# Two-layer gated network after a decayed linear attention on one core: outer products inside the values' product, a late check of the decay, and other options for the planner

## The chip, the core and the metric

The kernel runs on one core of a Trainium2 chip. The metric is the device time of one execution in microseconds (us). The kernel before takes 942.81 us (median of 3 runs, 942.36 to 943.93).

## What is computed

Three parts follow each other; the sizes are 4 batches of 768 positions, 8 heads of 48, a model width of 384 and a hidden width of 2048.

```python
for t in range(S):                       # attention, state per batch and head: 48 x 48
    cur = einsum('bhd,bhe->bhde', u * kt, vt)
    y[:, :, t] = einsum('bhd,bhde->bhe', rt, state + cur)
    state = w * state + einsum('bhd,bhe->bhde', kt, vt)
x = y laid out as (3072 tokens, 384)
h = x @ w_in;  x = (h * tanh(softplus(h))) @ w_out          # first layer
h = x @ w2_in; P = a0 + a1*h + a2*h^2 + a3*h^3              # second layer
Q = 1 + |b0|*|h| + |b1|*h^2;  out = (P / (Q + 1e-6)) @ w2_out
```

## The kernel before, in words

The 768 positions are cut into 6 chunks of 128. A **unit** is one chunk of one batch, so there are 24 units (`unit`, L619). A unit loads `kraw`, `rraw`, `tr` and `tkv`, scales them with powers of the decay (`L630`, `L633`, `L635`, `L653`), makes scores (TensorE, L646), puts a diagonal into `am` (L660, L663) and the scores over it (VectorE, L668), multiplies with the state (L679) and the values (L685), copies the result `y` (L464 on ScalarE, L467 on VectorE), moves it by DMA into `xr` and splits it into a high and a low part (`xh`, `xl`) of the reduced float type in which TensorE multiplies. For all but the last four units, eight outer products (`kv`, L705) follow, which update the state `st` (VectorE, L714 or L717).

The network runs in **steps** (`step`, L760 on): one step is one block of 512 tokens and one slice of 128 of the 2048 hidden columns. There are 198 steps, numbered from 0 here; the first 12 have half a block (256 tokens). A step has nine matmuls into `h` (L779, "first product"), a chain of VectorE and ScalarE work that ends in a high part `gh` and a low part `gl`, and nine matmuls into the accumulators `acc` (L855, "second product"). In the first layer the chain is clip `e` (VectorE, L794), four activations (ScalarE, L798), the product `h` (VectorE, L800), `gh` (L464 on ScalarE or L467 on VectorE) and `gl` (VectorE, L804). In the second layer it is `x`, `v`, `yy` (ScalarE, L809 to L814), `v*x` (GpSimd, L817), `x` and `h` (ScalarE, L819, L827), the products L821 to L835 on VectorE, and a split into `gh` and `gl` (L464 to L467 and L483).

Weights arrive as pairs of 32-bit words and are converted: one scaling (L58 on ScalarE, L60 on GpSimd), three VectorE instructions (L64, L67, L71), and a split into `w` high (L464) and `w` low (L483). The 16 slices of the first layer are converted in the first 200 us or so, beside the units.

Nothing of this order is written by hand. `Plan` collects every operation with the engines that may run it and a guessed cost, and lists them greedily: for each operation it takes the engine that would end it first, where an option may carry a handicap (fourth entry, for example the 3.0 in `(V, tt(n), True, 3.0)`), and among operations that could start within 0.1 of the earliest it takes the highest rank (longest way to the end, plus a `boost`). The engines then execute the list in order. Where TensorE would stand idle early in the list, `order` puts **zero products** (`filler`, L848: 512 columns times zeros into the first accumulator) into the gap, up to planned time `FILL`:

```python
if self.filler is not None and self.filler.done and st < self.FILL:
    y = free.get(e, 0.0)
    while y + (0.22 if clock.full else 0.44) < st:
        y = clock(y, 0.216, 1.0)
        order.append(self.filler)
```

At the very start of the list `check_decay` (L897) loads the decays and tests with four VectorE instructions (L902 to L905) whether they lie in a range; the result `fin` is read at the program's end. All DMAs are issued by SyncE (L459). At the end, three copies `o` of the accumulators (ScalarE, L464) go out by three DMAs.

Of the kernel before, what the change touches and what calls it, by code (L numbers as in the profile page):

```python
# [250 lines left out]
class Plan:  # L251
# [6 lines left out]
    FILL = 30.0  # L258
# [137 lines left out]
def tt(n):  # L396
    return 0.07 + 1.04e-3 * n


def ts(n):  # L400
    return 0.07 + 0.52e-3 * n


def act(n, src=0.093):
    return src + 0.833e-3 * n


def ptt(n):
    return 0.149 + 2.1e-3 * n
# [6 lines left out]
def fast_path(tc, nc, d):  # L416
# [40 lines left out]
    def dma(dst, src, r=(), w=(), nbytes=196608, after=(), boost=0.0):  # L457

        return pl.add([(SP, 0.65 if nbytes == 98304 else 0.5)], lambda e: nc.sync.dma_start(out=dst(), in_=src()),  # L459
                      r=r, w=w, lat=0.757, after=after, move=nbytes / 3.6e5, boost=boost)  # L460
# [8 lines left out]
    PV = 0.3  # L469
# [147 lines left out]
    AHEAD, AHEAD1 = 40.0, 10.0  # L617

    def unit(U):  # L619
# [52 lines left out]
        pv, y, xr = n_ps(), n_y(), n_xr()  # L672

        def values(e):

            for j in range(4 if c else 0):
                for i in range(2):
                    rows = slice(64 * i, 64 * i + D)
                    x_ = nc.tensor.matmul(pv()[64 * i:64 * i + D, j * CH:(j + 1) * CH],  # L679
                                          lhsT=st()[rows, j * D:(j + 1) * D], rhs=rraw()[rows, j, :],  # L680
                                          start=(j == 0), stop=False)
            for j in range(4):
                for i in range(2):
                    h = 2 * j + i
                    x_ = nc.tensor.matmul(pv()[64 * i:64 * i + D, j * CH:(j + 1) * CH],  # L685
                                          lhsT=tkv()[:, 384 + h * D:384 + (h + 1) * D], rhs=am[i]()[:, j, :],
                                          start=(j == 0 and c == 0), stop=(j == 3))
            return x_
        pl.add([(T, 2.1 if c else 1.1)], values, r=[tkv, rraw] + ([st] if c else []) + am, w=[pv], boost=bo,
               rows=0.8)  # L690
        pl.add([(A, act(512, 0.052)), (V, tt(512))],
# [6 lines left out]
        if not last:  # L698
            kp = n_ps()

            def kv(e):
                for j in range(4):
                    for i in range(2):
                        h = 2 * j + i
                        x_ = nc.tensor.matmul(kp()[64 * i:64 * i + D, j * D:(j + 1) * D],  # L705
                                              lhsT=tkv()[:, h * D:(h + 1) * D], rhs=tkv()[:, 384 + h * D:384 + (h + 1) * D],
                                              start=True, stop=True)
                return x_
            pl.add([(T, 0.5)], kv, w=[kp], r=[tkv], boost=bo, rows=0.75)
# [55 lines left out]
    def step(s, after):  # L765
# [4 lines left out]
        xh, xl = xt[blk]  # L770
        parts = range(3) if l else range(4) if half is None else range(2 * half, 2 * half + 2)
# [18 lines left out]
        if l == 0:  # L790
# [11 lines left out]
            pl.add([(A, act(n, 0.052)), (V, tt(n))], lambda e: copy(e, ghs(), hp()), r=[h], w=[gh])  # L802
# [3 lines left out]
        else:  # L806
# [9 lines left out]
            pl.add([(G, ptt(n)), (V, tt(n), True, 3.0)],  # L816
# [20 lines left out]
            split(n, g, ghs, gls, g, (gh, gl))  # L837
# [23 lines left out]
        if final:  # L861
            for m in range(3):
# [21 lines left out]
                if l == 0:  # L884
                    dma(lambda m=m: x2d[cb]()[:, m, :], o, r=[o], w=[(x2d[cb], m)], nbytes=262144)
                else:
                    dma(lambda m=m: d["out"][cb, :, m, :], o, r=[o], nbytes=262144)
# [9 lines left out]
    def check_decay():  # L897
# [8 lines left out]
        pl.add([(V, 1.7)], fn, w=[f0, f1])  # L906

    setup()
    check_decay()
# [7 lines left out]
    for s, (blk, f, half, *_) in enumerate(steps):  # L917
# [11 lines left out]
        step(s, [end])  # L929
    with tc.manual_schedule():  # L930
# [81 lines left out]
```

## Time and profile before

| What | Value |
|---|---|
| median of 3 runs | 942.81 us |
| the profiled execution, its own time | 946.39 us |
| its span, first to last instruction | 944.4 us |
| TensorE busy (matmuls) | 907.2 us, 96% |
| VectorE busy | 705.2 us, 75% |
| ScalarE busy | 723.2 us, 77% |
| GpSimd busy | 527.7 us, 56% |
| mean granted TensorE clock | 0.977 of full speed |

How to read it: TensorE is near its limit over the span as a whole, but the shares of an average over stages with different limits don't tell which stage has time left. The tables by stage and the single rows that matter stand further down. Names: PE is TensorE, PEld its weight loads, DVE VectorE, ACT ScalarE, POOL GpSimd, SP SyncE.

### The profile page before, as it was taken

The page shows a single profiled execution, that of the slowest core. Times are in us where ns is not written, and L with a number is a line of the kernel's source. Part 1 is how long each engine was busy: PE and PEld are TensorE (multiplying, and loading weights), DVE is VectorE, ACT ScalarE, POOL GpSimd, SP SyncE. Part 2 cuts the span into 40 slices and gives each one's busy share as a digit, 9 for nine tenths or more (in the row PEclk, how much of TensorE's full clock was granted, in tenths as well). Part 3 has the DMA queues.
Part 4 walks back from the last instruction along what each step waited for, and adds up shares of the span by engine and source line. Part 5 has one row for each costly group of instructions (what it writes and reads, how often), then busy time and mean ns, then how long its engine had stood idle before and what let it go on. Part 6 is the DMA issues. An engine that isn't in the chain of part 4 may idle for free. (4 is left out here: it accounts for less than half of the span.)

```text
span 944.4 us, 13963 instructions
## 1 busy us (share of the span) xinstructions
PE 907.2 (96%) x5009; PEld 739.6 (78%) x5009; DVE 705.2 (75%) x1072; ACT 723.2 (77%) x1256; POOL 527.7 (56%) x464
## 2 busy tenths in 40 slices
PE   6689899999999999999999999999999999999995
PEld 4578687788788788778888878888888888888883
DVE  7988998795544554544568999987878887878883
ACT  3556777676677677767788998997988988979784
POOL 2548644641810750330065597786877886867663
PEclk8769999999999999999999999999999999999999
DMA  8755357431500520330045310020100100100001
GB/s 311 247 176 176 122 168 233 130 99 47 176 10 1 174 84 1 84 98 1 0 156 169 111 62 6 1 68 1 56 12 1 56 12 1 56 1 1 34 1 37
DMA packets 38576, 75.11 MB, mean 80 GB/s; under 512 B 4322, under 2 KB 16739, under 8 KB 38499
## 3 DMA queue, kind: packets, MB, share of 16 engines
q1 hardware_dynamic: 38498, 74.14, 24.5%
q8 instruction: 41, 0.67, 0.3%
q14 instruction: 37, 0.30, 0.1%
HBM read 58.40 MB, written 11.01 MB: 73 GB/s over the span
## 5 line engine op out<-in xcount | busy, mean ns | idle before, releaser
L855 PE MATMUL acc<-gh,w 128*128 128x512 f32 (+1 forms) x1188 | 391.3, 388 | 1.9 <-DVE gh L467 1.0
L779 PE MATMUL h<-xh,w 128*128 128x512 f32 (+1 forms) x960 | 318.3, 389 | 6.5 <-DVE w L483 3.5
L798 ACT ACTIVATE e<-e 128x512 f32<-128x512 f32 (+1 forms) x408 | 245.7, 606 | 42.5 <-DVE e L794 34.5
L855 PEld LDWEIGHTS acc<-gh,w 128*128 128x128 f32 x1188 | 223.3, 190 | 49.2 <-ACT gh L464 2.2
L855 PE MATMUL acc<-gl,w 128*128 128x512 f32 (+1 forms) x594 | 229.7, 387 | 5.5 <-DVE gl L804 2.9
L779 PEld LDWEIGHTS h<-xh,w 128*128 128x128 f32 x960 | 181.5, 191 | 45.8 <-DVE w L483 4.8
L779 PE MATMUL h<-xl,w 128*128 128x512 f32 (+1 forms) x480 | 184.7, 385 | 0.0
L483 POOL TENSOR_TENSOR gl<-yy,gh 128x512 fp32r<-128x512 f32 x96 | 125.4, 1308 | 46.6 <-ACT gh L464 31.4
L817 POOL TENSOR_TENSOR v<-v,x 128x512 f32<-128x512 f32 x96 | 124.7, 1302 | 31.5 <-ACT v L811 17.9
L855 PEld LDWEIGHTS acc<-gl,w 128*128 128x128 f32 x594 | 112.7, 190 | 29.3 <-DVE gl L804 3.5
L800 DVE SCALAR_TENSOR_TENSOR h<-e,h 128x512 f32<-128x512 f32 (+1 forms) x102 | 67.4, 661 | 86.7 <-ACT e L798 86.4
L779 PEld LDWEIGHTS h<-xl,w 128*128 128x128 f32 x480 | 92.1, 192 | 16.8
L794 DVE TENSOR_SCALAR e<-h 128x512 f32<-128x512 f32 (+1 forms) x102 | 67.0, 657 | 38.2 <-PE h L779 38.0
L464 ACT ACTIVATE gh<-h 128x512 fp32r<-128x512 f32 (+1 forms) x91 | 52.9, 581 | 49.8 <-DVE h L800 48.4
L819 ACT ACTIVATE x<-v,ceps 128x512 f32<-128x512 f32 x96 | 69.6, 725 | 17.9 <-POOL v L817 17.8
L804 DVE TENSOR_TENSOR gl<-h,gh 128x512 fp32r<-128x512 f32 (+1 forms) x102 | 67.0, 657 | 16.1 <-ACT gh L464 12.6
L811 ACT ACTIVATE v<-x,cf 128x512 f32<-128x512 f32 x96 | 78.4, 817 | 0.0
L779 PE MATMUL aps<-xh,w 128*128 128x512 f32 x228 | 75.7, 389 | 0.0
L719 POOL TENSOR_TENSOR st<-st,pw 128x192 f32<-128x192 f32 x16 | 9.1, 573 | 94.5 <-DVE st L717 94.5
L829 DVE SCALAR_TENSOR_TENSOR v<-v,ceps,h 128x512 f32<-128x512 f32 x58 | 43.3, 746 | 24.1 <-ACT h L827 23.8
L663 ACT ACTIVATE am<-dmk,dg 128x128 f32<-128x128 f32 x100 | 31.8, 392 | 24.0 <-DVE dg L638 24.0
L779 PEld LDWEIGHTS aps<-xh,w 128*128 128x128 f32 x228 | 42.8, 188 | 8.9
(104 smaller groups left out, 1352.2 us busy)
## 6 DMA issues: line engine op xcount, KB each, us to landing
wr<-in_w SPq DMA_DIRECT2D x32, 768.0 KB, 4.3
tkv<-in_tkv SPq DMA_DIRECT2D x24, 384.0 KB, 4.0
kraw<-in_kT SPq DMA_DIRECT2D x24, 256.0 KB, 2.7
rraw<-in_rT SPq DMA_DIRECT2D x24, 256.0 KB, 3.6
x<-o SPq DMA_DIRECT2D x24, 256.0 KB, 2.5
o<-x SPq DMA_DIRECT2D x24, 256.0 KB, 2.9
tr<-in_tr SPq DMA_DIRECT2D x24, 192.0 KB, 2.8
xr<-y SPq DMA_DIRECT2D x48, 96.0 KB, 3.6
```

Of the source, the lines that this page charges most:

```text
L464: return nc.scalar.activation(out=out, in_=x, func=AF.Copy)
L483: lambda e: eng[e].tensor_tensor(out=lo(), in0=x(), in1=hi().bitcast(F32), op=ALU.subtract),
L779: x_ = nc.tensor.matmul(h()[:, :n], lhsT=w()[:, a, m, :], rhs=x()[:, m, col:col + n], start=(i == 0), stop=(i == 8))
L794: pl.add([(V, tt(n))], lambda e: nc.vector.tensor_scalar(out=es(), in0=hp(), scalar1=20.0, scalar2=None, op0=ALU.min), r=[h], w=[e_])
L798: lambda e, func=func, kw=kw: nc.scalar.activation(out=es(), in_=es(), func=func, **kw), w=[e_])
L800: lambda e: nc.vector.scalar_tensor_tensor(out=hp(), in0=es(), scalar=-0.5, in1=hp(), op0=ALU.add, op1=ALU.mult), r=[e_], w=[h])
L804: lambda e: nc.vector.tensor_tensor(out=gls(), in0=hp(), in1=ghs().bitcast(F32), op=ALU.subtract),
L811: lambda e: nc.scalar.activation(out=v(), in_=x(), func=AF.Identity, scale=cf()[:, 5:6], bias=cf()[:, 4:5]), r=[x, cf], w=[v])
L817: lambda e: eng[e].tensor_tensor(out=v(), in0=v(), in1=x(), op=ALU.mult), r=[x], w=[v])
L819: lambda e: nc.scalar.activation(out=x(), in_=v(), func=AF.Ln, bias=ceps()), r=[v, ceps], w=[x])
L829: lambda e: nc.vector.scalar_tensor_tensor(out=v(), in0=v(), scalar=ceps(), in1=h(), op0=ALU.add, op1=ALU.mult), r=[h, ceps], w=[v])
L855: x_ = nc.tensor.matmul(ac[m]()[:, col:col + n], lhsT=w()[:, a, 3 + m, :], rhs=x()[:, :n], start=(first and i == 0 and s > 0), stop=(final ...
```

## The change

- The eight outer products `kv` are no operation of their own any more: they stand at the end of the function `values`, behind the values' products, in one planned TensorE operation.
- The options of the copy `y` and of the first layer's `gh` give VectorE a handicap of 1.0 (`VA`), so ScalarE is taken unless VectorE would end it 1.0 earlier.
- `check_decay` is added behind step 48 and waits for that step's second product.
- `FILL` goes from 30 to 75; the rank boost of the second chunk's units (`AHEAD1`) from 10 to 0; two cost guesses of VectorE from 0.07 to 0.08.
- In the last steps (`end`, by the code steps 195, 196 and 197) the handicap of VectorE for `v*x` and for `gl` falls from 3.0 to 0.0 and 0.3.
- The second of the last three output DMAs is issued by ScalarE.

```diff
-    FILL = 30.0
+    FILL = 75.0
...
 def tt(n):
-    return 0.07 + 1.04e-3 * n
+    return 0.08 + 1.04e-3 * n
...
 def ts(n):
-    return 0.07 + 0.52e-3 * n
+    return 0.08 + 0.52e-3 * n
...
-        return pl.add([(SP, 0.65 if nbytes == 98304 else 0.5)], lambda e: nc.sync.dma_start(out=dst(), in_=src()),
+        return pl.add([(queue, 0.65 if nbytes == 98304 else 0.5)], lambda e: eng[e].dma_start(out=dst(), in_=src()),
...
-    PV = 0.3
+    PV, VA = 0.3, 1.0
...
-    AHEAD, AHEAD1 = 40.0, 10.0
+    AHEAD, AHEAD1 = 40.0, 0.0
...
         pv, y, xr = n_ps(), n_y(), n_xr()
+        kp = None if last else n_ps()
...
+            for j in range(0 if last else 4):
+                for i in range(2):
+                    h = 2 * j + i
+                    x_ = nc.tensor.matmul(kp()[64 * i:64 * i + D, j * D:(j + 1) * D],
+                                          lhsT=tkv()[:, h * D:(h + 1) * D], rhs=tkv()[:, 384 + h * D:384 + (h + 1) * D],
+                                          start=True, stop=True)
             return x_
-        pl.add([(T, 2.1 if c else 1.1)], values, r=[tkv, rraw] + ([st] if c else []) + am, w=[pv], boost=bo,
-               rows=0.8)
-        pl.add([(A, act(512, 0.052)), (V, tt(512))],
+        pl.add([(T, (2.0 if c else 1.0) + (0.0 if last else 0.4))], values, r=[tkv, rraw] + ([st] if c else []) + am,
+               w=[pv] + ([] if last else [kp]), boost=bo, rows=0.8)
+        pl.add([(A, act(512, 0.052)), (V, tt(512), False, VA)],
...
-            pl.add([(T, 0.5)], kv, w=[kp], r=[tkv], boost=bo, rows=0.75)
...
+        end = s > len(steps) - 4
...
-            pl.add([(A, act(n, 0.052)), (V, tt(n))], lambda e: copy(e, ghs(), hp()), r=[h], w=[gh])
+            pl.add([(A, act(n, 0.052)), (V, tt(n), False, VA)], lambda e: copy(e, ghs(), hp()), r=[h], w=[gh])
...
-            pl.add([(G, ptt(n)), (V, tt(n), True, 3.0)],
+            pl.add([(G, ptt(n)), (V, tt(n), True, 0.0 if end else 3.0)],
...
-            split(n, g, ghs, gls, g, (gh, gl))
+            split(n, g, ghs, gls, g, (gh, gl), early=end)
...
-                    dma(lambda m=m: d["out"][cb, :, m, :], o, r=[o], nbytes=262144)
+                    dma(lambda m=m: d["out"][cb, :, m, :], o, r=[o], nbytes=262144, queue=A if last and m == 1 else SP)
...
-    check_decay()
...
+        if s == 3 * NF:
+            check_decay([prev[1]])
```

What the planner makes of it is seen in three places. The line numbers of the changed kernel are 2 lower behind `check_decay`'s neighbours and in `step`, 12 lower for the outer products.

TensorE in the start-up, before: the fourth unit's last scores, its values' products and outer products, and then the first product of step 2 (`aps` are the PSUM banks of the units, `h_95` is that of the step).

```order
L646 MATMUL aps_92<-rraw,kraw 128x128
L646 MATMUL aps_93<-rraw,kraw 128x128
L685 MATMUL aps_92<-am,tkv 48x128 x8
L705 MATMUL aps_93<-tkv 48x48 x8
L779 MATMUL h_95<-xh,w 128x256
L779 MATMUL h_95<-xl,w 128x256
L779 MATMUL h_95<-xh,w 128x256 x2
L779 MATMUL h_95<-xl,w 128x256
L779 MATMUL h_95<-xh,w 128x256 x2
```

The same place now, from step 2's first product on.

```order
L777 MATMUL h_95<-xh,w 128x256
L777 MATMUL h_95<-xl,w 128x256
L777 MATMUL h_95<-xh,w 128x256 x2
L777 MATMUL h_95<-xl,w 128x256
L777 MATMUL h_95<-xh,w 128x256 x2
L777 MATMUL h_95<-xl,w 128x256
L777 MATMUL h_95<-xh,w 128x256
L846 MATMUL acc_154<-zer 128x512 x4
L686 MATMUL aps_92<-am,tkv 48x128 x8
L693 MATMUL aps_93<-tkv 48x48 x8
L846 MATMUL acc_154<-zer 128x512 x9
```

Step 2's first product now stands ahead of the fourth unit's values, and zero products stand on both sides of them. In all there are 52 zero products instead of 13.

VectorE in the start-up, before: from the clip of step 0 (`e<-h_96`) to its product (`h_96<-e,h_96`), with the check of the decay in between.

```order
L794 TENSOR_SCALAR e<-h_96 128x256
L714 TENSOR_TENSOR st_90<-aps_93,pw_81 128x192
L794 TENSOR_SCALAR e<-h_94 128x256
L902 TENSOR_SCALAR f_104<-f_103 1x384
L903 TENSOR_TENSOR f_103<-f_103,f_104 1x384
L904 TENSOR_REDUCE f_104<-f_103 1x1
L905 CAST fin<-f_104 1x1
L668 COPY_PREDICATED am<-msk,aps_92 128x512
L668 COPY_PREDICATED am<-msk,aps_93 128x512
L67 SCALAR_TENSOR_TENSOR wr<-wr 128x768
L638 TENSOR_REDUCE dg<-tr 128x8
L800 SCALAR_TENSOR_TENSOR h_96<-e,h_96 128x256
```

The same place now, on to the low part `gl` of step 0.

```order
L792 TENSOR_SCALAR e<-h_94 128x256
L67 SCALAR_TENSOR_TENSOR wr<-wr 128x768
L483 TENSOR_TENSOR w<-wr,w 128x768
L71 SCALAR_TENSOR_TENSOR wr<-wr 128x768
L668 COPY_PREDICATED am<-msk,aps_92 128x512
L668 COPY_PREDICATED am<-msk,aps_93 128x512
L798 SCALAR_TENSOR_TENSOR h_96<-e,h_96 128x256
L792 TENSOR_SCALAR e<-h_95 128x256
L64 TENSOR_SCALAR wr<-wr 128x768
L483 TENSOR_TENSOR w<-wr,w 128x768
L67 SCALAR_TENSOR_TENSOR wr<-wr 128x768
L802 TENSOR_TENSOR gl<-h_96,gh 128x256
```

The four instructions of the check are gone from here, `gh` is made elsewhere, and conversions of weights have moved up between the step's instructions.

ScalarE at the end, before: from the first operation on the last step's `h_96`.

```order
L809 ACTIVATE x<-h_96 128x512
L814 ACTIVATE yy<-h_96,cf 128x512
L819 ACTIVATE x<-v,ceps 128x512
L464 ACTIVATE gh<-yy 128x512
L827 ACTIVATE h_95<-x 128x512
L811 ACTIVATE v<-x,cf 128x512
L819 ACTIVATE x<-v,ceps 128x512
L464 ACTIVATE gh<-yy 128x512
L827 ACTIVATE h_96<-x 128x512
L464 ACTIVATE gh<-yy 128x512
```

The same place now.

```order
L807 ACTIVATE x<-h_96 128x512
L825 ACTIVATE h_95<-x 128x512
L812 ACTIVATE yy<-h_96,cf 128x512
L809 ACTIVATE v<-x,cf 128x512
L817 ACTIVATE x<-v,ceps 128x512
L825 ACTIVATE h_96<-x 128x512
L464 ACTIVATE gh<-yy 128x512
L464 ACTIVATE o<-acc_8172 128x512
L464 ACTIVATE o<-acc_8176 128x512
L464 ACTIVATE o<-acc_8180 128x512
L459 DMA out_x<-o 128x512
```

Between the last step's first activation and its `v`, two instructions of other steps are gone (`x` and a `gh`), and the `gh` between its last two activations too; the other step's `gh` is now made by GpSimd. One output DMA stands behind the last copy. On VectorE the last instruction is now the low part `gl` of step 197, and step 195's `gl` stands there too; `v*x` stays on GpSimd in all steps.

## Rows read from the trace of the kernel before

**Rows 1.** Busy time, clock and DMA share by stretch: busy us (instructions) per engine.

```profile
0.00:60.00 60.00, 41.50 (x292) 32.18 (x293) 53.40 (x97) 29.64 (x64) 27.41 (x31) 0.72 0.75 253
60.00:115.20 55.20, 49.78 (x474) 43.47 (x473) 46.76 (x80) 35.11 (x84) 34.88 (x31) 0.96 0.51 158
115.20:925.40 810.20, 807.89 (x4219) 659.14 (x4219) 599.77 (x890) 652.45 (x1100) 460.39 (x399) 1.00 0.20 62
...
20.00:30.00 10.00, 8.20 (x59) 5.58 (x57) 9.28 (x13) 4.63 (x9) 4.68 (x4) 0.66 0.97 323
```

**Rows 2.** Timeline of PE in the start-up: start, us, instruction [idle before <- releaser].

```profile
31.21 0.45 PE L685 MATMUL aps<-am,tkv 128*48 128x128 f32 x1 [2.61 <-DVE am L668]
...
115.12 0.53 PE L855 MATMUL acc<-gl,w 128*128 128x512 f32 x1 [0.69 <-DVE gl L804]
```

**Rows 3.** DVE groups by line, 0 to 120 us: xcount | busy us, mean ns.

```profile
L668 DVE COPY_PREDICATED am<-msk,aps 128x512 f32<-128x512 uint32 x18 | 12.4, 737 | 0.3 <-ACT am L663 0.3
L483 DVE TENSOR_TENSOR w<-wr,w 128x768 fp32r<-128x768 f32 x8 | 8.4, 1051 | 0.0
L630 DVE TENSOR_TENSOR kraw<-kraw,P_T 128x512 f32<-128x512 f32 x8 | 6.1, 761 | 0.5 <-DMA kraw<-in_kT 0.5
L635 DVE TENSOR_TENSOR tr<-tr,tkv 128x384 f32<-128x384 f32 x6 | 3.5, 581 | 1.4 <-DMA tkv<-in_tkv 1.4
L467 DVE COPY y<-aps 128x512 f32<-128x512 f32 x4 | 2.7, 682 | 0.4 <-PE aps L685 0.4
L467 DVE CAST gh<-h 128x256 fp32r<-128x256 f32 x5 | 2.1, 421 | 0.3
L804 DVE TENSOR_TENSOR gl<-h,gh 128x512 fp32r<-128x512 f32 x3 | 2.0, 681 | 0.0
L902 DVE TENSOR_SCALAR f<-f 1x384 f32<-1x384 f32 x1 | 1.5, 1465 | 0.0
L467 DVE CAST gh<-h 128x512 fp32r<-128x512 f32 x1 | 0.7, 692 | 0.0
L903 DVE TENSOR_TENSOR f<-f,f 1x384 f32<-1x384 f32 x1 | 0.5, 546 | 0.0
```

**Rows 4.** One weight conversion on DVE, whole span: ns min/median/max, first to last start.

```profile
L67 DVE SCALAR_TENSOR_TENSOR wr<-wr x32: 945/976/1771, 16.1 to 589.9; 128x768 int32<-128x768 int32 x32
```

**Rows 5.** PE timeline, an outer-product group alone, one joined, and values without one.

```profile
386.92 0.39 PE L855 MATMUL acc<-gl,w 128*128 128x512 f32 x1
387.15 0.39 PE L855 MATMUL acc<-gh,w 128*128 128x512 f32 x1
...
387.96 0.50 PE L779 MATMUL h<-xh,w 128*128 128x512 f32 x1
...
331.30 1.08 PE L685 MATMUL aps<-am,tkv 128*48 128x128 f32 x16
...
332.67 0.50 PE L855 MATMUL acc<-gh,w 128*128 128x512 f32 x1
...
402.24 1.08 PE L685 MATMUL aps<-am,tkv 128*48 128x128 f32 x16
403.25 0.50 PE L779 MATMUL h<-xh,w 128*128 128x512 f32 x1
```

**Rows 6.** Timeline of ACT and POOL over the last steps.

```profile
926.40 0.81 ACT L811 ACTIVATE v<-x,cf 128x512 f32<-128x512 f32 x1
929.25 0.61 ACT L464 ACTIVATE gh<-yy 128x512 fp32r<-128x512 f32 x1
933.58 1.26 POOL L483 TENSOR_TENSOR gl<-yy,gh 128x512 fp32r<-128x512 f32 x1 [2.37 <-ACT gh L464]
```

**Rows 7.** Output DMAs' issues (ns min/median/max), and the chain's last copy.

```profile
L459 SPq DMA_DIRECT2D out_x<-o x18: 333/382/1229, 616.6 to 938.3; - x18
...
937.04 0.60 ACT o L464
```

**Rows 8.** PE group of the zero products, 0 to 30 us: xcount | busy us, mean ns.

```profile
L848 PE MATMUL acc<-zer 128*128 128x512 f32 x13 | 5.7, 534 | 0.0
```

More of the change, by code (lines that the diff above doesn't have):

```diff
@@ L455, in bc, with dma @@
         return x[:, :, None].to_broadcast([x.shape[0], x.shape[1], n])
-    def dma(dst, src, r=(), w=(), nbytes=196608, after=(), boost=0.0):
-        return pl.add([(SP, 0.65 if nbytes == 98304 else 0.5)], lambda e: nc.sync.dma_start(out=dst(), in_=src()),
+    def dma(dst, src, r=(), w=(), nbytes=196608, after=(), boost=0.0, queue=SP):
+        return pl.add([(queue, 0.65 if nbytes == 98304 else 0.5)], lambda e: eng[e].dma_start(out=dst(), in_=src()),
                       r=r, w=w, lat=0.757, after=after, move=nbytes / 3.6e5, boost=boost)
@@ L698, in unit @@
         if not last:
[L699 to L708, printed above, removed]
-            pl.add([(T, 0.5)], kv, w=[kp], r=[tkv], boost=bo, rows=0.75)
             s4 = lambda: st()[:, 0:4 * D].rearrange("p (j e) -> p j e", j=4)
@@ L895, in x2, with check_decay @@
             split(512, o, lambda m=m: xh()[:, m, :], lambda m=m: xl()[:, m, :], o, ((xh, m), (xl, m)), boost=30.0)
-    def check_decay():
+    def check_decay(after):
         f0, f1 = fixed(cst, "f0", [1, H * D]), fixed(cst, "f1", [1, H * D])
@@ L905, in fn @@
             nc.vector.tensor_copy(fin, f1()[:, 0:1])
-        pl.add([(V, 1.7)], fn, w=[f0, f1])
+        return pl.add([(V, 1.7)], fn, w=[f0, f1], after=after)
     setup()
-    check_decay()
     end = None
```

## The prediction

> **What bounds the kernel now.** I read the table by stretch first [rows 1]. From 115.2 to 925.4 us TensorE is busy 807.9 of 810.2 us at full clock, so there only TensorE's own work counts, and nothing that another engine gains shortens the run. The time that can be won lies in three places. In the first 60 us TensorE is busy 41.5 us at a mean clock of 0.72, while VectorE is busy 53.4 us. From 60 to 115.2 us TensorE lacks 5.4 us (55.2 - 49.8). And behind 925.4 us comes an end in which the engines wait for each other in turn.
>
> Next the timeline of TensorE: the last wait of the start-up ends at 115.12 us and was for a low part `gl` that VectorE makes, the one of step 13 [rows 2]. From there TensorE runs through. So the time is, to first order, the moment at which this `gl` is ready, plus TensorE's remaining work, plus the end. VectorE reaches that `gl` after nearly unbroken work, so the question for the start-up is how much VectorE work the new order puts ahead of it.
>
> **Start-up: VectorE's work ahead of step 13's `gl`.** I counted VectorE's instructions in the two orders up to that row, and priced the difference with the groups' means [rows 3].
> - Gone to ScalarE: 4 copies `y` (4 x 0.682 = 2.73) and 6 high parts `gh` (5 x 0.421 + 0.692 = 2.80).
> - Gone to a later place: the check of the decay, 1.465 + 0.546 = 2.01 with its two long instructions (two shorter ones I leave out). Behind step 48 it stands where VectorE is idle a quarter of the time (599.8 busy of 810.2, [rows 1]), and only the program's end reads its result: no cost there. Its small DMA stays early in SyncE's queue.
> - Gone to GpSimd: 4 multiplications `kraw` (3.04) and 3 of `tr` (1.74).
> - Come from GpSimd: 2 multiplications `rraw`, at the price of `kraw` (1.52), and 1 low part of `w` (1.05).
>
> Together 12.32 - 2.57 = 9.75 us less. But the new order has also done more by that row: 2 copies into `am` (1.47) and a weight conversion (0.98, its median [rows 4]), less one clip, priced as the `gl` of its size (0.68). That leaves **8.0 us** by which `gl` of step 13 comes earlier, if VectorE idles as long as before.
>
> The two `am` copies belong to the ninth unit, whose products with state and values and outer products now also stand ahead of step 13 on TensorE; before they came behind it. From the start of a values' product to what follows is 403.25 - 402.24 = 1.01 us, the state's product has as many matmuls of the same width, so again 1.01, and the outer products add 0.36 (next part) [rows 5]. So **2.4 us** less of TensorE's work remains behind that point.
>
> Some of this will come back as new waits. Each `gh` on ScalarE puts a round trip between two VectorE instructions, and between 60 and 115 us TensorE itself is busy 90% already (49.8 of 55.2), so it cannot move far forward there. The bounds are no loss and the 5.4 us that TensorE lacks in that stretch now. I take 2.0 back, nearer to none: VectorE's rows for these instructions show 0.3 or 0.4 us idle ahead of a whole group [rows 3], so the order has other work to put between them.
>
> ScalarE gets some 5 us of copies there at the prices above; it is busy 29.6 of 60 and 35.1 of 55.2 us [rows 1], so this is hidden, and would cost its length if ScalarE were full.
>
> **Zero products.** 39 more, a mean of 0.44 us each before (5.7 / 13) [rows 8]. They stand in planned gaps. Three of the 13 of before stand directly ahead of the values' products of 31.21 us, and TensorE still waited 2.61 us behind them for `am` [rows 2]: the real engines ran later than the list expected, and the products ended before anyone needed TensorE. I cost them at nothing; the cover is VectorE's lateness.
>
> **Outer products in the saturated stretch.** Alone, a group costs 387.96 - 387.15 = 0.81 us less the 0.23 that two regular matmuls are apart, so 0.58. Behind the values it adds 1.37 - 1.01 = 0.36 [rows 5]. The difference is 0.22. In the order of before 9 of 20 groups stand alone, 7 of them behind 115 us; now none. That is TensorE's own time: **1.5 us** less. Their later place does not hurt there: `st` is needed only by the next chunk's unit.
>
> **The end.** The last step's `v` began at 926.40 us, behind two other steps' instructions that the new order puts ahead of its first activation, and its second last activation waited 0.5 us for the `gh` of 929.25 us, which is now GpSimd's. The last `gl` took GpSimd 1.26 us [rows 6]; VectorE makes one in 0.68 [rows 3], so 0.6 is sure. Of the order on ScalarE I count 0.9, as the instructions moved ahead may delay that first activation. `v*x` stays on GpSimd. Together **1.5 us**, between 0.6 and 2.0.
>
> The last copy ended at 937.64 us, but its DMA was issued only at 938.3 us, as the issue of the DMA before it held SyncE for 1.23 us [rows 7]. Now ScalarE issues that one, behind the last copy, so the last one starts **0.6 us** earlier. The bounds are a gain of 0.7, and a loss of 0.6 if ScalarE's issue takes such a 1.2 us in its turn.
>
> **The sum:** -8.0 - 2.4 + 2.0 - 1.5 - 1.5 - 0.6 = -12.0 us. The profiled execution took 946.39 us, so it would take 934.4; it lay 3.6 us above the median of the runs, 942.81, from which I expect **930.8 us**.
>
> **Rival 1, slower: zero products in the way.** They are in the list, not made when needed. 34 of the 52 now stand between just ahead of step 2's first product and that of step 5. If the real engines are not late there, a released operation queues behind them: 39 x 0.44 = 17.2 us, less the 12.0, gives 948.0 us. It decides from the point where `am` or a `gh` is ready before its group of zero products ends. Against it: the 2.61 us of waiting behind such a group [rows 2]. For it: VectorE, whose lateness hides them, is what gets faster. 7%.
>
> **Rival 2: GpSimd takes it back.** A weight conversion on VectorE took 0.945 us at best and 1.771 at worst [rows 4], so something holds it up by 0.83 at times. If each of the 7 multiplications that went to GpSimd does that once, 5.8 us return: 936.6 us. For it: the bad ones lie in the start-up. Against it: GpSimd also gives work away there. The Trainium skill, page "SBUF — State Buffer", section "Who interferes with whom", says that a VectorE instruction with two SBUF inputs and a GpSimd instruction that reads SBUF exclude each other for the whole instruction. By that rule, these moves are not free, and this rival's time is what it would make; the spread of rows 4 agrees with it. 20%.
>
> **Rival 3: the clock comes up too.** TensorE's mean clock is 0.96 from 60 to 115 us [rows 1]; full clock there gives 4% of 55.2, 2.2 us more: 928.6 us. Against it: between 20 and 30 us the clock was 0.66 although zero products stood there. The Trainium skill, page "TensorE: Matmul & The Clock Gate", section "HAM oscillation — how this bites in real kernels", says that idle stretches put the clock back to its lower level, so that the work behind them starts slowly. By that rule filled gaps keep it at 2.4 GHz and this rival's time holds; the 0.66 agrees only in part. 15%.
>
> **Rival 4: transfers bound the start-up.** The DMA engines were 97% busy from 20 to 30 us [rows 1]. If they hold up VectorE as soon as it is faster, the start-up gains nothing and 3.6 us remain: 939.2 us. Against it: the share is 0.51 from 60 us on. 7%.
>
> **Rival 5: it doesn't do what it says.** A new order may open a wait elsewhere that eats the gain, within 0.2% of before. 3%.
>
> **How the numbers follow.** The forecast has 48%. The range goes from 925.5 (rival 3, without the 2.0 taken back, and the bound of the end) to 939.5 us (rival 4), and leaves out rival 1 and the edges. A measurement of this kernel can tell 0.2% (1.9 us) from no change. Forecast and rivals 2, 3 and 4 are faster by more; with some doubt within each: faster 0.88, the same 0.05, slower 0.07.
>
> **What would show it.** Right: step 13's `gl` is ready near 107 us and no longer TensorE's last wait by much; VectorE's groups of `gh` and `y` are gone from the start-up; the last low part stands on VectorE with 0.7 us; no outer products between regular matmuls. Wrong: TensorE waits in the first 115 us about as long as before, zero products run while `am` is long ready, or the saturated stretch from there to the end has new idle time.

## The result, and the profile after

The changed kernel takes 934.42 us (median of 6 runs, 932.57 to 938.01) against 943.37 us for the kernel before on the same chip (6 runs, 942.23 to 945.16): a ratio of 0.9911, 95% interval 0.9886 to 0.9937. The medians lie 9.0 us apart, and the ratio makes it 8.4 us. The time is inside the range, and 3.6 us above the forecast of 930.8 us. The profiled execution took 932.57 us, the lowest of the six, its span 930.9.

The table by stretch of the changed kernel, beside [rows 1] (columns as there: stretch, its length, busy us of PE, PEld, DVE, ACT, POOL, granted clock, DMA share, GB/s):

```profile
0.00:60.00 60.00, 46.63 (x365) 37.22 (x365) 54.05 (x94) 33.86 (x75) 24.30 (x30) 0.89 0.80 276
60.00:115.20 55.20, 51.61 (x510) 44.18 (x510) 48.77 (x77) 42.75 (x100) 40.19 (x34) 1.00 0.54 168
115.20:912.00 796.80, 794.59 (x4139) 650.39 (x4138) 590.46 (x877) 645.19 (x1098) 453.65 (x392) 1.00 0.19 61
```

TensorE is busier, in part with zero products, and its clock is higher in both early stretches. VectorE is busy 102.8 us up to 115.2 (54.05 + 48.77), where it was 100.2 before (53.40 + 46.76, [rows 1]). But by then the changed kernel is further on, so this says nothing of VectorE's work. The fair stretch ends with the same instruction, the `gl` of step 13, which VectorE finishes at 115.07 us before and at 108.05 us now (before, then changed):

```profile
0.00:115.07 115.07, 91.20 (x763) 75.57 (x763) 100.03 (x176) 64.65 (x147) 62.16 (x62) 0.84 0.64 208
0.00:108.05 108.05, 91.09 (x815) 75.44 (x817) 96.79 (x160) 69.58 (x162) 59.62 (x59) 0.94 0.68 229
```

Up to there VectorE is busy 3.2 us less (100.03 - 96.79), where the prediction counted 8.0, and idle 3.8 us less (15.0 to 11.3). The timeline of TensorE in the changed kernel, beside [rows 2]:

```profile
48.47 0.39 PE L777 MATMUL h<-xh,w 128*128 128x256 f32 x1 [1.87 <-DVE gl L802]
...
109.64 0.50 PE L853 MATMUL acc<-gh,w 128*128 128x512 f32 x1
109.97 0.39 PE L853 MATMUL acc<-gl,w 128*128 128x512 f32 x1
...
918.19 0.50 PE L853 MATMUL acc<-gh,w 128*128 128x512 f32 x1 [1.02 <-POOL gh L466]
919.55 0.50 PE L853 MATMUL acc<-gl,w 128*128 128x512 f32 x1 [0.85 <-POOLq L941]
...
922.00 0.50 PE L853 MATMUL acc<-gl,w 128*128 128x512 f32 x1
```

Step 13's second product no longer waits: its `gl` is ready 1.9 us before TensorE comes to it. Behind step 195, two waits are left, for step 196's `gh` and `gl`, which GpSimd makes.

Where the time went is seen best at fixed points. By the first product of step 12 both orders have done the same work on TensorE, except the zero products and one group of outer products more in the changed one; by that of step 34 the changed one has also made the scores of one unit more; by that of step 197 all but the zero products is the same. Starts in us, read from the timelines ("again": the two repeats below):

| | before, profiled | before again | changed, profiled | changed again |
|---|---|---|---|---|
| step 12's first product | 96.44 | 94.14 | 88.62 | 88.38 |
| step 34's first product | 208.36 | 204.81 | 199.11 | 199.42 |
| step 197's first product | 921.35 | 917.66 | 910.22 | 911.82 |
| TensorE's last product ends | 937.00 | 933.32 | 924.11 | 926.90 |
| span | 944.4 | 939.9 | 930.9 | 933.9 |

Between the two repeats 5.8 of 6.0 us are there by step 12. Between the two executions profiled first, a slow one of before and the fastest of the changed kernel's, it is 7.8 of 13.5.

### The profile page after: what moved, and what is told of

Same layout as the page of the kernel before. It is cut to its first block, busy times and chain, and to the rows that moved or that the text cites. A ratio compares the mean times of both kernels' runs of the same rounds, so it can differ in the third digit from the quotient of the medians.

```text
span 930.9 us, 14046 instructions
## 1 busy us (share of the span) xinstructions
PE 902.6 (97%) x5048; PEld 738.3 (79%) x5048; DVE 700.1 (75%) x1055; ACT 728.9 (78%) x1282; POOL 522.3 (56%) x458
## 4 chain that ended last, share of the span: by engine, by line
PE 83%; DVE 6%; ACT 4%; DMA 3%; issue 1%; POOL 1%; SPq 1%; ACTq 0%; POOLq 0%; DVEq 0%
PE acc L853 38%; PE h L777 30%; PE aps L777 8%; PE aps L646 2%; DMA wr<-in_w 2%; PE aps L686 2%; PE aps L680 2%; ACT e L796 2%; DVE wr L71 1%; DVE wr L67 1%; DVE wr L64 1%; DVE w L483 1%; DMA kraw<-in_kT 1%; SPq L459 1%; DMA tkv<-in_tkv 1%
## 5 line engine op out<-in xcount | busy, mean ns | idle before, releaser
L853 PE MATMUL acc<-gh,w 128*128 128x512 f32 (+1 forms) x1188 | 387.3, 385 | 2.3 <-ACT gh L464 1.3
L777 PE MATMUL h<-xh,w 128*128 128x512 f32 (+1 forms) x960 | 312.9, 384 | 3.7 <-DVE w L483 1.9
L777 PEld LDWEIGHTS h<-xh,w 128*128 128x128 f32 x960 | 178.5, 188 | 41.5 <-DVE w L483 2.7
L483 POOL TENSOR_TENSOR gl<-yy,gh 128x512 fp32r<-128x512 f32 x94 | 123.1, 1310 | 34.3 <-ACT gh L464 23.8
L777 PEld LDWEIGHTS h<-xl,w 128*128 128x128 f32 x480 | 90.2, 188 | 17.6 <-DVE xl L483 0.7
L464 ACT ACTIVATE gh<-h 128x512 fp32r<-128x512 f32 (+1 forms) x102 | 58.1, 570 | 42.4 <-DVE h L798 40.6
L630 POOL TENSOR_TENSOR kraw<-kraw,P_T 128x512 f32<-128x512 f32 x20 | 28.2, 1412 | 101.6 <-DMA kraw<-in_kT 101.6
L819 DVE TENSOR_TENSOR yy<-yy,h 128x512 f32<-128x512 f32 x58 | 39.6, 683 | 10.9 <-ACT yy L812 10.5
```

The costliest lines, as they stand in the source:

```text
L464: return nc.scalar.activation(out=out, in_=x, func=AF.Copy)
L483: lambda e: eng[e].tensor_tensor(out=lo(), in0=x(), in1=hi().bitcast(F32), op=ALU.subtract),
L777: x_ = nc.tensor.matmul(h()[:, :n], lhsT=w()[:, a, m, :], rhs=x()[:, m, col:col + n], start=(i == 0), stop=(i == 8))
L853: x_ = nc.tensor.matmul(ac[m]()[:, col:col + n], lhsT=w()[:, a, 3 + m, :], rhs=x()[:, :n], start=(first and i == 0 and s > 0), stop=(final ...
```

## Experiments

**Both kernels once more, unchanged.** The prediction rests on one profile of before, 3.6 us above the median.

> The changed kernel itself, once more. By the theory of the sum (8.0 us of VectorE's work gone ahead of step 13's low part) its gain is a property of the order, so this profile shows TensorE at step 13's second product at about 109.6 us again and the time within 1 us of 934.4. Rival: the six runs from 932.6 to 938.0 differ because the start-up falls out differently each time (transfers, the granted clock); then this profile's start-up differs by over 1 us, and the difference sits before 115 us.

> The kernel before, once more. The profiled execution of the prediction took 946.39 us, 3 us over the median of the runs. Theory: these 3 us lay in the start-up, a longer stretch at half clock or later transfers, so part of what the sum was taken from isn't there in an ordinary run; then this profile, if it takes 942 to 944 us, has the last wait of the start-up at 111 to 113 us instead of 115.1. Rival: they lie elsewhere (the end, the launch), and step 13 is at 114 to 115 us again.

The changed kernel: 936.00 us, ratio 0.9926 (0.9898 to 0.9953), its start-up as before (step 13's second product at 109.66), its time 1.6 us over the 934.4. The kernel before: 943.82 us, ratio 1.0003 (0.9980 to 1.0027), profiled at 941.57, with the last wait of the start-up ending at 112.54. The table shows where the two profiles of before part: 2.3 us by step 12, 3.6 by step 34, 3.7 at step 197, 4.5 in the span. So most of what sets the execution that I worked from apart lay in the start-up, the very stretch that the change rebuilds, and 0.8 behind it at the end. VectorE's busy time up to step 13's `gl` is no smaller in the repeat (101.6 us), but it idles 10.9 us there instead of 15.0.

Every ratio here and below is to the kernel before, run in the same round on the same chip (its medians: 943.15, 944.07 and 943.43 us); times of different rounds come from different chips.

**Is it VectorE's load? The check back early; the ten copies back on VectorE.** Both keep the changed kernel's order; the first moves the check of the decay to where it stood, behind step 1's clip, the second runs four copies `y` and six `gh` on VectorE.

```diff
...
+        ops.remove(check)
+        ops.insert(next(i for i, op in enumerate(ops) if op.what == "e1") + 1, check)
...
```

```diff
-            (self.fill if op in made else op.fn)(op.eng)
+            (self.fill if op in made else op.fn)("V" if op.what == "V" else op.eng)
...
```

> The changed kernel with its order kept on every engine, but the four VectorE instructions of the decay's check back behind the second clip, where they stood before. Theory (VectorE bounds the start-up): 2.0 to 2.7 us slower than the changed kernel, all of it ahead of step 13. Rival (the waits between the engines take it up): under 1 us slower.

> The changed kernel with its order kept, but the 4 copies y and the 6 high parts that VectorE made in the start-up before are VectorE's again, at the places where ScalarE makes them now. Theory (VectorE bounds the start-up): 5.5 us slower (2.73 + 2.80). Rival 1 (half of it is taken up by waits, as each copy on VectorE also saves a round trip to ScalarE): 2 to 3 us slower. Rival 2 (TensorE bounds): under 1 us.

936.60 us (ratio 0.9921, 0.9896 to 0.9945) and 935.78 us (0.9925, 0.9895 to 0.9954), against 936.00: the 2.01 us of the check cost 0.6 in the median and 1.0 at step 12 (89.40 against 88.38), the 5.53 us of the copies nothing in the median (0.2 less) and 0.5 at step 12 (88.85). The intervals, over 2 us to either side, leave room for such small costs, not for 5.5. So two terms that made up 7.5 of the 12.3 us counted off VectorE are worth about 1.5 together at step 12, in one profile each.

This doesn't show that VectorE's load is without effect, because its load hardly rose. Up to step 13's `gl` it is busy 97.3 us with the check and 97.5 with the ten copies, against 96.7: 0.6 and 0.8 more, not 2.0 and 5.5. With the copies there, VectorE's other instructions took some 4 us less, above all the conversions (L64 8.4 instead of 9.7 us, L67 11.8 instead of 12.3) and the two `xl` (1.2 instead of 2.7). Why they got shorter no run has separated.

**Is it the order? The boost alone.** One number of the kernel before (`AHEAD1` 10 to 0), and the changed kernel with that number put back, both planned anew.

```diff
-    AHEAD, AHEAD1 = 40.0, 10.0
+    AHEAD, AHEAD1 = 40.0, 0.0
```

> The kernel before with one number changed, the rank boost of the second chunk's units from 10 to 0, and planned anew. Theory: the start-up gain is made by the order that this boost sets (step 2's first product ahead of the fourth unit's values, fewer waits of TensorE ahead of step 4). Then step 12's first product, 94.1 us in the kernel before run again and 88.4 in the changed one run again, starts at 88 to 91 us, and the time falls by 3 to 6 us (ratio 0.994 to 0.997). Rival: the order needs the copies on ScalarE, the late check and the joined outer products as well; then it stays at 93 to 96 us and the ratio is 0.999 to 1.002.

> The changed kernel with that boost back at 10, planned anew; everything else of the change stays. Theory of the order: step 12's first product falls back to 92 to 95 us and the time to 939 to 942 us (3 to 6 more than the changed kernel run again, 936.0). Rival (the other parts make the gain): it stays within 1 us of 88.4 and the time at 935 to 937 us.

The boost alone: 938.98 us, ratio 0.9955 (0.9940 to 0.9969), 4.5 us below before, where the change is 9.0 below in its first runs and 7.2 in the repeat. Step 12's first product starts at 91.28 us, just behind the 88 to 91 expected. That of step 34, with the same work done, starts at 197.31 instead of 204.81 us, and the changed kernel run again had 199.42: up to there the boost alone gains at least as much as the whole change, in one profile each. From there to step 197 it loses 3.8 us (716.7, against 712.9): 1.1 are longer waits, 1.7 are 3.4 us at 1.2 GHz from 540.0 us on, and 1.0 stays unexplained. VectorE's timeline shows one thing that moved. Kernel before (run again), from step 0's product `h` to its low part `gl`:

```profile
43.47 0.43 DVE L800 SCALAR_TENSOR_TENSOR h<-e,h 128x256 f32<-128x256 f32 x1
...
44.91 0.41 DVE L467 CAST gh<-h 128x256 fp32r<-128x256 f32 x1
...
49.17 1.48 DVE L630 TENSOR_TENSOR kraw<-kraw,P_T 128x512 f32<-128x512 f32 x1
50.58 1.48 DVE L630 TENSOR_TENSOR rraw<-rraw,P_T 128x512 f32<-128x512 f32 x1
51.98 0.54 DVE L638 TENSOR_REDUCE dg<-tr 128x8 f32<-128x384 f32 x1
52.44 0.41 DVE L804 TENSOR_TENSOR gl<-h,gh 128x256 fp32r<-128x256 f32 x1
```

The same place with the boost at 0, and below it TensorE's wait for this `gl` in either (first before, then with the boost at 0):

```profile
44.29 0.42 DVE L800 SCALAR_TENSOR_TENSOR h<-e,h 128x256 f32<-128x256 f32 x1
...
45.43 0.94 DVE L483 TENSOR_TENSOR w<-wr,w 128x768 fp32r<-128x768 f32 x1
46.29 0.94 DVE L67 SCALAR_TENSOR_TENSOR wr<-wr 128x768 int32<-128x768 int32 x1
47.16 0.41 DVE L804 TENSOR_TENSOR gl<-h,gh 128x256 fp32r<-128x256 f32 x1
```

```profile
52.90 0.58 PE L855 MATMUL acc<-gl,w 128*128 128x256 f32 x1 [4.25 <-DVE gl L804]
```

```profile
47.62 0.58 PE L779 MATMUL h<-xh,w 128*128 128x256 f32 x1 [0.60 <-DVE gl L804]
```

In the order before, `gh` is ready at 45.32 us and `gl` begins at 52.44: the multiplications of a unit of the second chunk (the sixth `kraw` in order of time) stand between. Without the boost they stand behind it, and TensorE's wait for this `gl` goes from 4.25 to 0.60 us (now ahead of a later step's first product). In all it waits 16.3 us up to step 12 instead of 20.4, and 0.2 from there to step 34 instead of 4.0. In the changed kernel the same interval looks like this, VectorE first, then GpSimd:

```profile
42.70 0.44 DVE L798 SCALAR_TENSOR_TENSOR h<-e,h 128x256 f32<-128x256 f32 x1
...
44.34 2.07 DVE L483 TENSOR_TENSOR w<-wr,w 128x768 fp32r<-128x768 f32 x1
46.33 1.75 DVE L67 SCALAR_TENSOR_TENSOR wr<-wr 128x768 int32<-128x768 int32 x1
48.00 0.41 DVE L802 TENSOR_TENSOR gl<-h,gh 128x256 fp32r<-128x256 f32 x1
```

```profile
43.96 1.62 POOL L630 TENSOR_TENSOR kraw<-kraw,P_T 128x512 f32<-128x512 f32 x1
45.55 1.71 POOL L653 TENSOR_TENSOR tkv<-tkv,P_t 128x384 f32<-128x384 f32 x1
```

`h` is 1.6 us earlier than with the boost alone, and `gl` 0.8 later: two conversions took 3.82 us that took 1.88 there.

Of the second run, the changed kernel with the boost at 10, neither expectation held whole: 937.32 us, ratio 0.9934 (0.9912 to 0.9957), 1.3 above the changed kernel run again. Step 12's first product falls back to 93.48 us as the theory had it, but TensorE waits no more up to there (13.3 us in all, against 13.7). In its place run zero products, of which the planner put 70 into this order. Groups of PE up to 95 us, this run and then the changed kernel run again:

```profile
L846 PE MATMUL acc<-zer 128*128 128x512 f32 x70 | 22.2, 452 | 0.0
```

```profile
L846 PE MATMUL acc<-zer 128*128 128x512 f32 x52 | 17.0, 455 | 0.0
```

They are 5.2 us more, about the 5.1 by which step 12 is later. Whether they delay it or only fill waits is not shown, as no run leaves them out; VectorE too is later, with 99.9 us of work up to step 13's `gl`, 3.2 more than in the changed kernel run again. Step 0's `gl` is not the reason, since here it is ready earliest of all:

```profile
44.43 0.42 DVE L802 TENSOR_TENSOR gl<-h,gh 128x256 fp32r<-128x256 f32 x1
```

From step 12 to step 34 this run wins 3.5 back (107.5 us, against 111.0). So the boost alone gives 4.5 us, and the rest of the change without it 6.1, of 7 to 9: the two overlap. Which other part makes those 6.1, with the boost at 10, no run has separated.

**Are the zero products hidden?** The 34 late ones left out, and doubled, in the changed kernel's order.

```diff
             if op in made:
                 zeros += 1
                 if zeros > 18:
-                    continue
+                    self.fill(op.eng)
```

(The line with the minus is the first run, the one with the plus the second.)

> The changed kernel with its order kept, but without the 34 zero products that stand behind the first 18, that is from just ahead of step 2's first product on. Theory 1 (VectorE's work bounds the start-up, zero products are hidden and change nothing): within 1 us of the changed kernel, which took 936.0 us here. Theory 2 (from 53 to 88 us TensorE bounds, and the zero products keep its clock up): the granted clock falls to half somewhere between 35 and 65 us, the first product of step 12 starts 2 to 5 us later than 88.4 us, and the time is 2 to 5 us longer.

> The changed kernel with its order kept and each of those 34 zero products made twice. Theory (they lie in waits that are there anyway): the first half cost nothing; of 34 more at 0.22 us (7.3 us at full clock) some 2 us go into the remaining waits, so 5 us slower, and step 12's first product starts 5 us later. Rival (VectorE bounds that stretch): 0 to 2 us slower, as TensorE catches up behind it.

Left out: 936.37 us, ratio 0.9913 (0.9892 to 0.9935), step 12's first product at 88.31: no difference. Doubled: 939.82 us, ratio 0.9954 (0.9937 to 0.9972), step 12 at 92.29, 3.9 later. They are hidden as they are, but the cover ends soon behind them. In these two profiles the clock differs. TensorE from 39.8 to 53.5 us (busy us, granted clock, DMA share, GB/s), without the late ones and then in the changed kernel:

```profile
39.80:53.50 13.70, 9.59 (x62) 0.50 0.73 228
```

```profile
39.80:53.50 13.70, 11.66 (x92) 1.00 0.72 226
```

At 1.2 GHz the real products of this stretch were still done in time, since TensorE waits for VectorE there (3.0 us for step 0's `gl`, which frees it at 48.64).

**What do outer products alone cost?** The groups of 12 units put alone in the changed kernel, and all groups joined to the values in the kernel before, each in its own order.

```diff
-            for j in range(0 if last else 4):
+            for j in range(4 if c < 2 else 0):
...
+            if held and op.eng == "T":
+                held("T")
```

```diff
+            if isinstance(op.what, tuple) and op.what[0] == "kv":
+                continue
...
+            if isinstance(op.what, tuple) and op.what[0] == "values" and op.what[1] in outer:
+                outer[op.what[1]].fn("T")
```

> The changed kernel with its order kept, but the outer products of the 12 units of the third to fifth chunk stand alone, behind TensorE's next operation. By the row prices 12 x 0.22 = 2.6 us slower, all between 115 and 430 us. Rival (the update of the state, now later, holds up a later unit, or the matmuls of other engines' waits hide it): 0 or over 4 us.

> The kernel before in its own order, with each group of outer products directly behind its unit's values' products (9 of 20 stood alone). Theory from the rows of the run with the groups alone: a group alone costs 0.33 us more than one behind the values (0.32 to enter it instead of 0.10, and 0.10 in the first regular product behind it), so 3.0 us of TensorE's time for 9 groups, 2.3 of them behind step 13: from step 34's first product to the end 1.3 to 1.7 less for the 5 groups behind it or so, ratio 0.996 to 0.998. By the price of the prediction, 0.22, it is 2.0 in all, ratio 0.998. Rival: the 8.6 us of that run were only waits and the clock; then the ratio is 0.999 to 1.001.

Alone: 944.60 us, ratio 1.0012 (0.9998 to 1.0027), 8.6 more than the changed kernel run again (8.1 by the two ratios), against 2.6 by the price of the prediction. The timeline of TensorE in that run shows what the price left out:

```profile
233.25 0.39 PE L869 MATMUL acc<-gh,w 128*128 128x512 f32 x1
233.57 0.56 PE L687 MATMUL aps<-tkv 128*48 128x48 f32 x16
234.06 0.50 PE L793 MATMUL h<-xh,w 128*128 128x512 f32 x1
234.40 0.39 PE L793 MATMUL h<-xl,w 128*128 128x512 f32 x1
```

The group takes 0.58 us as I had it (234.06 - 233.25 - 0.23), but the regular matmul behind it is 0.34 from the next instead of 0.23. Behind the values that 0.11 is paid anyway. So a group alone costs 0.58 + 0.11 - 0.36 = 0.33 us, not 0.22.

Joined, in the kernel before: from step 34's first product to that of step 102, 4 groups were alone. It took 322.52 us in both profiles of before, and 321.43 in this run, with one new wait of 0.23: 1.32 us less, 4 x 0.33. The whole kernel did not gain, 945.42 us, ratio 1.0014 (0.9991 to 1.0036). Its profile shows a late start-up, with step 12 at 96.84 us and step 34 at 208.99, near the first profile of before. The wait for step 0's `gl` is no measure of that: it is 5.1 us here, and 2.2 and 4.25 in the two profiles of before, of which the second starts step 12 earlier. From step 12 to step 34 TensorE waited 5.0 us in all, where it was 3.8 and 4.0, and ran 3.4 us at 1.2 GHz. So the 0.33 is shown between steps 34 and 102, not in the kernel's time.

Between the same two steps the run with the groups alone took 331.2 us, the changed kernel run again 324.2. Of these 7.0 us, 2.6 are 8 groups at 0.33, 1.3 are longer waits (3.1 against 1.9), and 1.7 are 3.4 us at 1.2 GHz from 497.6 us on; 1.4 stay unexplained.

**The end.** The changed kernel with its last `gl` back on GpSimd and the DMA back on SyncE; and the changed kernel with 7 zero products in the two waits for step 196.

```diff
...
+            e = "G" if op.what == "gl197" else "S" if op.move and op.eng == "A" else op.eng
...
```

```diff
+                    for _ in range((4, 3, 0)[i] if s == len(steps) - 2 and m == 0 else 0):
+                        nc.tensor.matmul(ac[0](), lhsT=zer(), rhs=zer()[:, None, :].to_broadcast([CH, 4, CH]),
+                                         start=False, stop=False)
```

> The changed kernel with its order kept, but step 197's low part is GpSimd's again, and the second of the last three output DMAs SyncE's. By the prediction's terms 0.6 us from the last low part to TensorE's end, and 0.6 us from there to the end of the span: 1.2 us slower in the profile from step 197's first product on. Rival (ScalarE's own issue cost as much): no difference behind TensorE's last matmul.

> The changed kernel in its own order with 7 zero products more at the end, 4 ahead of step 196's second product and 3 behind its first matmul, where TensorE waited 1.02 and 0.86 us for GpSimd's gh and gl and the granted clock then fell to half for 3.4 us in most of the profiles. Theory: the clock stays full there, and from step 197's first product to TensorE's last product it takes 13.9 us, as in the one profile without the fall, instead of 15.0 to 15.1; the median is 0.5 to 1.2 us below the changed kernel run again (936.0). Rival: the clock falls all the same, and the zero products at half clock come late for gh; then 15.1 us or more, and no gain or a loss of up to 1 us.

Undone: 938.32 us, ratio 0.9932 (0.9913 to 0.9951). From step 197's first product to TensorE's end its profile takes 15.10 us, the changed kernel run again 15.08, and the step from there to the end of the span is 6.8 us in this run, 6.8 and 7.0 in the two profiles of the changed kernel. Neither part of the end shows there. For the first, the clock is the reason: GpSimd's last `gl` is ready at 927.67 us and TensorE, behind 3.4 us at 1.2 GHz, comes to it only at 928.21. In the changed kernel's first profile, at full clock, it came 0.05 us behind VectorE's. The changed kernel run again, from step 197's first product on (TensorE alone):

```profile
911.82:921.50 9.68, 7.43 (x31) 1.00 0.00 0
921.50:924.90 3.40, 3.40 (x10) 0.50 0.01 5
924.90:926.90 2.00, 2.00 (x9) 1.00 0.03 8
```

Behind the waits of 1.02 and 0.86 us for step 196, the clock is at 1.2 GHz for 3.4 us. Of the nine profiles with these two waits (the changed kernel's two, and those of the check, the copies, the zero products left out and doubled, the groups alone, the end undone and the boost at 10) six have this; three, the first one above among them, have not. With the zero products in these waits:

```profile
919.64 1.07 PE L854 MATMUL acc<-zer 128*128 128x512 f32 x4
920.80 0.50 PE L856 MATMUL acc<-gh,w 128*128 128x512 f32 x1
921.14 0.87 PE L854 MATMUL acc<-zer 128*128 128x512 f32 x3
922.18 0.50 PE L856 MATMUL acc<-gl,w 128*128 128x512 f32 x1 [0.17 <-POOLq L944]
```

```profile
922.50:925.90 3.40, 3.32 (x15) 1.00 0.01 2
```

The clock stays at 2.4 GHz, and the end takes 13.89 us. As it did so in three of nine profiles without them too, one profile doesn't settle that the zero products are the cause. The median is 933.87 us (932.48 to 936.04), ratio 0.9897 (0.9875 to 0.9920), the lowest of all versions. It is 2.1 us below the changed kernel run again and 0.6 below its first runs; these intervals overlap, so it is not settled that it beats the change.

## Why the prediction was right or wrong

**The sum and its base.** -12.0 us from the profiled execution's 946.39 gives 934.4, and the kernel takes 934.42, but that match is in part luck: the two executions profiled first are 13.8 us apart, the two repeats 5.9, the medians 9.0 and 7.2. What failed is the last step, "it lay 3.6 us above the median of the runs, 942.81, from which I expect 930.8 us". That treats the surplus as something beside the change. The repeat of before, at 941.57 us somewhat below its own median, has 3.6 us less to lose by step 34, and against it the change wins 5.8 us at step 12 (94.14 to 88.38), not the 7.8 that the first profiles show.

**Start-up, -8.0 -2.4 +2.0.** The size came out between the first profiles and not between the repeats: TensorE's product with step 13's `gl` starts at 109.97 us instead of 115.12, or 110.00 instead of 112.54, in either case with 2.4 us more of the units' work done, so 7.6 and 5.0 us against the 8.4. The sign named for it is there, this `gl` being ready at 108.05 us and waited for no longer. The step that failed is the price, "priced the difference with the groups' means". It holds every other instruction at the length it had. VectorE's busy time up to that `gl` fell by 3.2 us (100.0 to 96.8), and by 4.9 between the repeats (101.6 to 96.7), not by 8.0, because what was left got longer, `w` above all. In the first pair VectorE also idled 3.8 us less, which the prediction had put at no change. That is luck: the repeat of before idles 10.9 us there and the changed kernel run again 11.4.

What in the new order makes the gain is only in part shown. The boost, which had no term of its own but is in the count of instructions, gives all of it up to step 34 when it is changed alone. The rest of the change gives much of it too, with the boost where it was. How early step 0's `gl` is ready doesn't decide it. Whether VectorE's work bounds the start-up, as the prediction has it, stays open: its busy time up to step 13's `gl` goes with the time at which that is ready in most runs (95.1 and 106.7 us with the boost alone, 99.9 and 112.5 with it at 10), but the run meant to add 5.5 us to it added 0.8, and with the zero products doubled it is busy 94.3 us and that `gl` comes at 111.20, so there TensorE bounds.

**Zero products, 0.** Right, and for the reason given, VectorE's lateness. Rival 1's mechanism is real: doubled, they cost 3.9 us at step 12.

**GpSimd takes it back (rival 2).** The mechanism is there, and it is what the start-up's price left out. Groups of VectorE in the changed kernel from 0 to 120 us, beside [rows 3], and the conversion over the whole span, beside [rows 4]:

```profile
L483 DVE TENSOR_TENSOR w<-wr,w 128x768 fp32r<-128x768 f32 x10 | 13.4, 1342 | 0.0
L630 DVE TENSOR_TENSOR kraw<-kraw,P_T 128x512 f32<-128x512 f32 x4 | 3.8, 956 | 0.0
```

```profile
L67 DVE SCALAR_TENSOR_TENSOR wr<-wr x32: 942/968/2017, 15.7 to 578.9; 128x768 int32<-128x768 int32 x32
```

One `w` takes 0.29 us more than before, 2.9 us over ten. That is most of the 4.8 us between the 8.0 counted and the 3.2 that VectorE's busy time fell; the rival had 5.8. How much of it reaches the kernel's time no run has separated. The Trainium skill, page "SBUF — State Buffer", section "Who interferes with whom", says that a VectorE instruction with two SBUF inputs contends with a GpSimd instruction that reads SBUF, and that this is an exclusive lock. The rows at 44 to 48 us above agree in kind: 2.07 and 1.75 us beside GpSimd's multiplications. In the run with the boost alone both took 0.94, and there GpSimd's multiplication beside them took 3.47 (last section).

**The clock comes up too (rival 3).** It did: it is full from 34.4 us on, and in the run without the late zero products it was at half from 39.8 to 53.5 us. The Trainium skill, page "TensorE: Matmul & The Clock Gate", section "HAM oscillation — how this bites in real kernels", says that idle stretches put the clock back to its lower level. That run agrees in kind: TensorE is busy 2.0 us from 36.4 to 39.8 us, ahead of the fall; but the changed kernel is busy no more from 44.6 to 48.0 us and keeps its clock. At step 12 the full clock gave no time, as TensorE was not what the stretch waited for; and the 0.96 from 60 to 115 us, on which the 2.2 us rested, was that execution's own: in the repeat of before it is 1.00.

**Transfers (rival 4) and the range.** The start-up did gain, with the DMA share at 0.80 in the first 60 us where it was 0.75, so transfers did not hold that back. The lower bound of 925.5 does not come out of the terms named for it, which give 926.0.

**Outer products, -1.5.** Right in kind; by the runs above a group is worth 0.33, not 0.22, so an estimated 2.3 us for the seven. I took the distance to the next matmul and left out that this matmul itself takes 0.50 instead of 0.39 us, which the rows showed [rows 5].

**The end, -1.5, and the DMA, -0.6.** The last `gl` is on VectorE and took 0.69 us. From step 197's first product to TensorE's end 15.65 us became 13.89 at full clock, 1.8 less, but 15.08 where the clock falls, 0.6 less; that fall had no place in the term. The DMA's 0.6 was a 1.23 us issue [rows 7] that does not come each time. In the changed kernel, and in the run with the end undone:

```profile
L459 SPq DMA_DIRECT2D out_x<-o x17: 332/393/462, 604.8 to 924.8; - x17
L459 ACTq DMA_DIRECT2D out_x<-o x1: 376/376/376, 924.2 to 924.2; - x1
```

```profile
L460 SPq DMA_DIRECT2D out_x<-o x18: 332/403/488, 609.9 to 931.1; - x18
```

With all 18 on SyncE none took more than 0.49 us here; the longest was 0.72 in the repeat of before and 1.20 with the boost alone. From TensorE's end to the end of the span it takes 7.4 and 6.5 us in the two profiles of before, 6.8 and 7.0 in those of the changed kernel: no gain is shown, and the 0.7 of the first pair is the long issue.

**New idle time in the middle.** As feared in small: TensorE waits for step 91's `gh` and `gl` (0.7 us in all in the first profile, 1.9 in the repeat) and for step 112's `gl` (1.26), where before it waited 1.9 for step 107 alone. In the repeat that is 1.2 us more, about what the four groups joined there win (1.3); in the first profile it is 0.1.

## What to carry to other kernels

A price list of the instructions that move holds only while the others keep their length. After the change, compare an engine's busy time up to the same instruction in both kernels, not up to the same time: here 8.0 us counted off were 3.2 to 4.9. The same holds for a run that puts work back: see first whether the busy time rose by what was added. A profiled execution that is slower than the median has its surplus somewhere: profile the same kernel again before subtracting it, because a change that rebuilds that stretch may have taken it already. And a short group of narrow matmuls costs more than its own length: compare the duration of the first regular one behind it.

## What was not expected of the hardware

Two waits of 1.0 and 0.9 us, half a microsecond apart, were followed by 3.4 us at 1.2 GHz in 6 of 9 profiles, and with 7 matmuls on zeros in them the clock stayed at 2.4 GHz in the one execution profiled. Ten copies put on VectorE, 5.5 us by their own rows, raised its busy time up to the same instruction by 0.8 us only. And where VectorE and GpSimd work side by side, it can be GpSimd's multiplication that takes long and not VectorE's instruction, as far as the profile's rough times of GpSimd go. In the run with the boost alone GpSimd needed 3.47 us for `kraw`, where its mean in the changed kernel is 1.41, while VectorE's `w` and conversion beside it took 0.94 each:

```profile
44.90 3.47 POOL L630 TENSOR_TENSOR kraw<-kraw,P_T 128x512 f32<-128x512 f32 x1
```
